# Building the convolution bands by columns, and reordering the loads and first factors of the head, in a fused convolution and FFN kernel

## The chip, the cores and the metric

The kernel runs on one core of one Trainium2 chip. The metric is device time in microseconds (us) of one execution; lower is better. PE is TensorE, DVE is VectorE, ACT is ScalarE, POOL is GpSimd and SP is SyncE; PE has its own row, PEld, for weight loads.

## The reference

`x` has shape (8, 3904, 192) and `weight` has shape (8 heads, 7 taps). Each head owns 24 of the 192 channels.

```python
w = softmax(weight, axis=-1)                      # per head, over the 7 taps
x_pad = 6 rows of zeros ahead of each of the 8 sequences
out[b, s, h, g] = sum_k w[h, k] * x_pad[b, s + k, h, g]
x = out.reshape(31232, 192)
h = ((x @ w1) * (x @ w2)) @ w3                    # w1, w2: 192 x 1024; w3: 1024 x 1024
return h @ w_out                                  # w_out: 1024 x 192; float32
```

## The kernel before

The 31232 tokens are handled as two streams of 15616 (`r` = 0, 1), 64 partitions each. A chunk `R` has `CH` = 512 tokens of each stream, so there are 31 chunks, the last one of 256; four chunks form a group and there are eight groups. The program is written in the order in which each engine executes it: there is no scheduler, and each engine's queue follows the order of the Python calls.

**Convolution.** A window is 64 input rows that give 58 outputs (`Q` = 64, `ST` = 58, `PAD` = 6). `conv` (L416) multiplies a window with a 64 x 64 band matrix per head, which holds the seven softmaxed taps on its diagonals; the bands lie in `Aband`. Windows come in blocks `b` of 6, 4, 8, 10, 8, 20, 20 and 14; `xb` holds a block's inputs, `convo` its outputs, and `xT` the transposed tokens that TensorE needs next. Blocks 0 to 4 are transposed on TensorE (`pe_transpose`, L470, and `joint_transposes`, L629), later ones go through `rows` in memory and are transposed by DMA. `EARLY` is 6 x 58 = 348, the tokens of block 0.

**FFN.** `wd[0]` and `wd[1]` hold w1 and w2 in bf16, twice, once for each stream's 64 partitions. For each of eight tiles `ft` of 128 columns, `first_factor` (L500) makes the factor a = x @ w1 (i = 0) and b = x @ w2 (i = 1) into a pair of PSUM banks. `first_cast` (L508, ACT) copies a to `asb`, `first_times` (L519, DVE) multiplies it with b into `abT`. w3 @ w_out is made once (`W_sb`, L590), and `second_product` (L551) multiplies `abT` with it. ACT copies the result to `osb` (L556), which a DMA stores (L566, L559).

**PSUM** is four pairs of banks in a list: `banks()` takes the first, `drained(p)` appends it again. A matmul into a pair waits for the copy that emptied it.

**The head**, up to about 40 us, in the order in which it is issued:

- SP loads the first quarter (256 columns) of both weights as float32 into `wfirst` (L176, two DMAs).
- POOL issues the input loads, which also convert to bf16: rows 1 to 5 of block 0 (L184), the first window's rows (L194, two DMAs of 58 rows), block 1 (L131, two), the second quarter of w1 and w2 (L181, two) and so on. Between these loads stand POOL's own operations: a select that makes `diag` (L188), a conversion of a part of `wfirst` (L198), and, as a DMA fills only partitions 0 to 63 of `wd`, copies of each quarter to partitions 64 to 127 (`copy_w`, L202).
- PE runs matmuls on zeros (`warm`, L218), six of 512 columns first.
- DVE and ACT make the softmax, PE spreads the taps over the partitions (L242, then L244 copies them).
- `band` (L259, L268) makes the bands in four steps of two heads: DVE writes a product of `diag` and the taps (128 x 448), 28 matmuls with `ident` add up its seven diagonals, and ACT or DVE copies the result to `Aband` (L602).
- ACT converts `wfirst` between these copies (L198, three times), POOL the fourth part.
- The convolution of block 0 follows (L416, L599), its transposes, the convolution of block 1, then `first_part(0, [0], 0, EARLY)`, the transposes of block 1, `first_part(0, [1], 0, EARLY)`, then tokens 348 to 511 of both tiles, and tiles 2 to 7 with the convolutions of blocks 2 to 4 between them.

**The tail**: in the last group `second_product` stores chunk 28 with one DMA per stream, chunk 29 with four, and the last chunk in parts.

Of the kernel before, what the change touches and what calls it, by code (L numbers as in the profile page):

```python
# [8 lines left out]
FP32 = mybir.dt.float32  # L9
BF16 = mybir.dt.bfloat16  # L10
AX = mybir.AxisListType
ALU = mybir.AluOpType
# [4 lines left out]
def kernel(  # L17
# [10 lines left out]
    nc = tc.nc  # L28
# [125 lines left out]
    wfirst = work.tile([Q, 2, NP, DFF // 4], FP32, tag="abT", bufs=GROUP, name="wfirst")  # L154
# [4 lines left out]
    half = const.tile([1, 3 * Q], BF16)  # L159
    ident = const.tile([128, 128], BF16)  # L160
    diag = const.tile([128, Q + PAD], BF16)
    nc.vector.memset(zeros, 0.0)
    nc.vector.memset(tiny, 0.0)
    nc.vector.memset(ones, 1.0)
    nc.vector.memset(xb0[:, 0, :], 0.0)
    nc.vector.memset(half, 0.0)
    nc.vector.memset(half[:, Q:2 * Q], 1.0)
    nc.vector.memset(ident, 0.0)
# [9 lines left out]
    def load_w(part):  # L178
        cs = slice(WC[part], WC[part + 1])
        for i in range(2):  # L180
            nc.gpsimd.dma_start(out=wd[i][0:Q, :, cs], in_=w_rows[i][:, :, cs])  # L181

    def load_x0(r):
        nc.gpsimd.dma_start(out=xb0[Q * r:Q * r + Q, 1:, :], in_=x_spans(r, 1, 2 * n0 - 1))  # L184

    load_x0(0)
    for p0 in (0, Q):
        nc.gpsimd.affine_select(  # L188
            out=diag[p0:p0 + Q], in_=ones[p0:p0 + Q].to_broadcast([Q, Q + PAD]),
            pattern=[[-1, Q + PAD]], compare_op=ALU.is_equal, fill=0.0, base=0,  # L190
            channel_multiplier=1)
    load_x0(1)
    for r in range(NS):
        nc.gpsimd.dma_start(out=xb0[Q * r + PAD:Q * r + Q, 0, :],  # L194
                            in_=x_rows[r * TS:r * TS + ST, :])
    load_x(1)
    def cast_w(i, r, f):
        f(out=wd[i][Q * r:Q * r + Q, :, 0:WC[1]], in_=wfirst[:, i])  # L198

    def copy_w(part, i, f):  # L200
        cs = slice(WC[part], WC[part + 1])
        f(out=wd[i][Q:128, :, cs], in_=wd[i][0:Q, :, cs])  # L202

    load_w(1)
    cast_w(1, 1, nc.gpsimd.tensor_copy)
    load_w(2)
    load_x(2)
    for i in range(2):
# [3 lines left out]
        copy_w(2, i, nc.gpsimd.tensor_copy)  # L212
    load_x(3)

    def warm(n):
        p, t = banks()
        for j in range(n):
            nc.tensor.matmul(t[:, j % 2, :], zeros, zeros[:, 0:1].to_broadcast([128, CH]),  # L218
                             start=True, stop=True)
        drained(p)  # L220

    warm(6)

    wmax = const.tile([1, H], FP32)
    wsum = const.tile([1, H], FP32)
    wrow = const.tile([1, H, K], BF16)
    wsb = const.tile([128, 2, 2, K], BF16)
# [3 lines left out]
    nc.scalar.activation(out=wall, in_=wall, func=ACT.Exp)  # L231
    nc.vector.tensor_copy(out=ident[0:Q, 0:Q], in_=diag[0:Q, 0:Q])
    nc.vector.reduce_sum(out=wsum, in_=wall, axis=AX.X)
    nc.vector.reciprocal(out=wsum, in_=wsum)
    nc.vector.tensor_tensor(
        out=wrow, in0=wall, in1=wsum.unsqueeze(2).to_broadcast([1, H, K]), op=ALU.mult)
    nc.vector.tensor_copy(out=ident[Q:128, Q:128], in_=diag[Q:128, 0:Q])
    pw, wbc = banks()
    wbc = wbc[:, 0, 0:H * K // 2].rearrange("p (g e k) -> p g e k", g=2, e=2)
    wrow = wrow.rearrange("p (g e a) k -> p g e a k", g=2, a=2)  # L240
    for a in range(2):
        nc.tensor.matmul(wbc, half[:, Q - Q * a:Q - Q * a + 128], wrow[:, :, :, a],  # L242
                         start=(a == 0), stop=(a == 1))
    nc.vector.tensor_copy(out=wsb, in_=wbc)  # L244
    drained(pw)
    warm(2)

    Aband = const.tile([128, 2, 2, 2, Q], BF16)

    def band_of(h, r):  # L250
        return Aband[Q * r:Q * r + Q, h // 4, (h % 4) // 2, int(h % 2 != r), :]

    d0 = diag[:, 0:1]
    taps = bass.AP(tensor=d0.tensor, offset=d0.offset,
                   ap=[list(d0.ap[0]), [1, K], [1, Q]])

    def band(g, e):
        c = slot([128, K, Q], BF16, "cprod")
        nc.vector.tensor_tensor(  # L259
            out=c, in0=taps, in1=wsb[:, g, e].unsqueeze(2).to_broadcast([128, K, Q]),  # L260
            op=ALU.mult)
        p, bps = banks()
        for k in range(K):
            for v in range(2):
                for r in range(2):
                    rs = slice(Q * r, Q * r + Q)
                    o = Q * (r ^ v)
                    nc.tensor.matmul(bps[o:o + Q, v, 0:Q], ident[rs, rs], c[rs, k, :],  # L268
                                     start=(k == 0), stop=(k == K - 1))
        return p, Aband[:, g, e], bps[:, :, 0:Q]  # L270


    shared, held, VHEADS = {}, [], (3, 4, 6, 7)

# [217 lines left out]
    def first_factor(R, i, fts, c0, c1):  # L492
        n, r0 = c1 - c0, (R * CH) % RING
        assert len(fts) * n <= CH
        q, p = banks()
        for e, ft in enumerate(fts):
            for k in range(NP):
                for r in range(NS):
                    rs = slice(Q * r, Q * r + Q)
                    nc.tensor.matmul(  # L500
                        p[:, r, e * n:e * n + n], wd[i][rs, k, ft * 128:(ft + 1) * 128],
                        xT[k][rs, r0 + c0:r0 + c1], start=(k == 0), stop=(k == NP - 1))
        return q, p[:, :, 0:len(fts) * n]
# [97 lines left out]
    def put(f, p, dst, src):  # L601
        f(out=dst, in_=src)  # L602
        drained(p)

    cast_w(0, 0, A)
    put(A, *band(0, 0))
    put(A, *band(0, 1))
    cast_w(0, 1, A)
    made = [band(1, 0), band(1, 1)]
    put(V, *made[0])  # L610
    put(V, *made[1])
    cast_w(1, 0, A)

    def move_all(p, moves, fs):
        for f, m in zip(fs, moves):
            move(f, m)
        drained(p)
# [38 lines left out]
    first_part(0, [0, 1], EARLY, CH)  # L656
    load_w3(0)
    for i in range(2):
# [87 lines left out]
    for p in SHARED:  # L746
# [76 lines left out]
```

## Time and profile before

| | |
|---|---|
| median of three runs | 514.25 us (513.17 to 515.23) |
| time of the profiled execution | 512.8 us |
| its span in the profile | 511.1 us |
| PE busy | 505.2 us (99%) |
| DVE, ACT, POOL busy | 421.5, 358.3, 340.1 us |
| the chain that ended last | PE 96%, DVE 2%, ACT 1% |

The page divides the span into engines and groups of instructions; a line's number, as in L500, is that of the kernel before. A row of the timeline has the start, the time that the merged instructions took, the engine, the line, what is written and read, how many there were, and in brackets how long the engine had been idle and what ended that. An engine's name with a q is its queue at an instruction that only issues.

### The profile page before, as it was taken

Reading aid. Unit: us, or ns where it says so; the run is one execution under the profiler, and the core shown is the slowest. Engines: PE = TensorE matmul, PEld = TensorE weight load, DVE = VectorE, ACT = ScalarE, POOL = GpSimd, SP = SyncE. Lnnn points to the kernel's source line nnn. Section 1 sums busy time; section 2 is a strip of 40 time slices with the busy share of each in tenths; the row PEclk is TensorE's granted clock in tenths of the full one; section 3 lists DMA queues with packets and bytes.
Section 4 is the critical chain, followed back from the end, with each engine's and each line's share of the span. In section 5 each row is a group of like instructions: output and inputs, shape, how many; then the busy total and the mean of one; then the engine's idle time right before and its main releaser. Section 6 shows DMA issues by size and latency. Waiting matters only on the chain.

```text
span 511.1 us, 13682 instructions
## 1 busy us (share of the span) xinstructions
PE 505.2 (99%) x5608; PEld 343.4 (67%) x5608; DVE 421.5 (82%) x482; ACT 358.3 (70%) x479; POOL 340.1 (67%) x437
## 2 busy tenths in 40 slices
PE   8999999999999999999999999999999999999997
PEld 4554798555985559855598555985559855597487
DVE  6889624999959999699998999989999899983970
ACT  6787645777857777477785777857778577765762
POOL 8601535449979999899985999969999594030000
PEclk9999999999999999999999999999999999999999
DMA  9999999995692989687926898467963683036104
GB/s 120 165 172 122 169 179 228 153 211 81 93 257 88 138 112 193 217 132 63 124 95 185 155 120 102 119 192 149 116 78 107 190 139 63 2 118 183 27 3 156
DMA packets 135188, 67.91 MB, mean 133 GB/s; under 512 B 99050, under 2 KB 133411, under 8 KB 135061
## 3 DMA queue, kind: packets, MB, share of 16 engines
q0 software_dynamic: 48720, 29.05, 40.1%
q1 hardware_dynamic: 86259, 37.89, 35.3%
q8 instruction: 44, 0.72, 0.6%
q14 instruction: 19, 0.16, 0.1%
q10 hardware_dynamic: 146, 0.10, 0.1%
HBM read 39.60 MB, written 36.56 MB: 149 GB/s over the span
## 4 chain that ended last, share of the span: by engine, by line
PE 96%; DVE 2%; ACT 1%; issue 0%; ACTq 0%; DVEq 0%
PE pairs L500 61%; PE pairs L551 32%; PE pairs L416 2%; PE pairs L590 1%; DVE abT L519 1%; ACT asb L508 1%; PE pairs L218 1%; DVE cprod L259 0%; PE pairs L629 0%; ACT convo L437 0%; PE pairs L470 0%; DVE xT L642 0%; DVE convo L599 0%; PE pairs L268 0%; ACT osb L556 0%
## 5 line engine op out<-in xcount | busy, mean ns | idle before, releaser
L519 DVE TENSOR_TENSOR abT<-asb,pairs 128x1024 bf16<-128x1024 bf16 (+1 forms) x245 | 298.0, 1217 | 31.3 <-ACT asb L508 14.1
L500 PE MATMUL pairs<-xT,wd 64*128 64x512 bf16 (+3 forms) x3000 | 319.4, 371 | 0.5 <-DVE xT L642 0.2
L508 ACT CAST asb<-pairs 128x1024 bf16<-128x1024 f32 (+1 forms) x245 | 247.3, 1009 | 66.7 <-PE pairs L500 66.6
L500 PEld LDWEIGHTS <-wd 64*128 64x128 bf16 x3000 | 164.9, 94 | 149.2 <-issue 1.4
L551 PE MATMUL pairs<-W_sb,abT 128*128 128x192 bf16 x1952 | 163.3, 246 | 0.0
L551 PEld LDWEIGHTS <-abT 128*128 128x128 bf16 x1952 | 160.4, 98 | 3.7 <-issue 3.7
L556 ACT COPY osb<-pairs 128x384 f32<-128x384 f32 x122 | 57.7, 476 | 73.1 <-PE pairs L551 72.1
L347 POOL TENSOR_TENSOR acc<-acc,term 128x480 f32<-128x480 f32 (+2 forms) x90 | 92.9, 1032 | 7.1
L344 POOL TENSOR_TENSOR term<-xv,wv 128x480 f32<-128x480 bf16 (+2 forms) x114 | 97.5, 856 | 0.0
L329 DVE SCALAR_TENSOR_TENSOR pairs<-xv,wv,pairs 128x480 f32<-128x480 bf16 (+2 forms) x120 | 76.6, 638 | 5.0 <-ACT pairs L327 1.6
L347 POOL TENSOR_TENSOR terms<-terms 128x480 f32<-128x480 f32 (+2 forms) x30 | 31.0, 1034 | 29.4 <-ACT terms L300 27.8
L437 DVE CAST convo<-pairs 128x672 bf16<-128x672 f32 (+9 forms) x29 | 20.4, 752 | 33.7 <-PE pairs L416 17.2
L338 POOL TENSOR_TENSOR acc<-xv,wv 128x480 f32<-128x480 bf16 (+2 forms) x18 | 15.7, 872 | 13.8 <-DMA xv<-in_x_dram 13.4
L350 POOL TENSOR_TENSOR y<-acc,term 128x240 bf16<-128x240 f32 (+7 forms) x48 | 22.8, 502 | 1.4
L300 ACT ACTIVATE terms<-xv,wv 128x480 f32<-128x480 bf16 (+2 forms) x36 | 20.6, 625 | 0.0
L332 DVE SCALAR_TENSOR_TENSOR y<-xv,wv,pairs 128x240 bf16<-128x240 bf16 (+2 forms) x48 | 18.1, 420 | 1.1
L384 POOL DMA_DIRECT2D rows<-y x10 | 5.7, 572 | 19.6 <-issue 17.5
L461 POOL DMA_DIRECT2D rows<-convo x10 | 6.0, 604 | 17.2 <-ACT convo L437 16.6
L131 POOL DMA_DIRECT2D xb<-in_x_dram x20 | 13.9, 721 | 3.4 <-PE pairs L590 2.7
L327 ACT ACTIVATE pairs<-xv,wv 128x480 f32<-128x480 bf16 (+2 forms) x24 | 14.0, 597 | 1.1 <-DVE y L332 1.1
L359 POOL DMA_DIRECT2D xb<-in_x_dram x20 | 14.7, 756 | 0.0
L279 POOL DMA_DIRECT2D xv<-in_x_dram x12 | 13.5, 1128 | 1.4 <-DMA rows<-convo 1.2
(70 smaller groups left out, 113.5 us busy)
## 6 DMA issues: line engine op xcount, KB each, us to landing
out_dram<-osb SPq DMA_DIRECT2D x50, 384.0 KB, 3.2
xv<-in_x_dram POOLq DMA_DIRECT2D x6, 768.0 KB, 9.6
out_dram<-osb POOLq DMA_DIRECT2D x8, 384.0 KB, 4.9
xv<-in_x_dram POOLq DMA_DIRECT2D x4, 672.0 KB, 13.7
xb<-in_x_dram POOLq DMA_DIRECT2D x16, 168.0 KB, 6.4
rows<-y POOLq DMA_DIRECT2D x3, 720.0 KB, 6.3
w3rows<-in_moe_w_dram POOLq DMA_DIRECT2D x2, 1024.0 KB, 12.1
xb<-in_x_dram POOLq DMA_DIRECT2D x8, 240.0 KB, 6.3
```

The lines of the kernel that those rows point to most:

```text
L300: nc.scalar.activation(out=term.rearrange("p (m g) -> p m g", g=G), in_=xv[:, k:k + W].rearrange("p s r c -> p (s r) c")[:, :, h * G:h * G ...
L329: f.scalar_tensor_tensor(out=flat, in0=xs(k), scalar=tap(k), in1=flat, op0=ALU.mult, op1=ALU.add)
L332: f.scalar_tensor_tensor(out=dst, in0=xv[:, 0:W, r, h * G + cs.start:h * G + cs.stop], scalar=tap(0), in1=by_row[:, :, r, cs], op0=ALU.mul ...
L344: f.tensor_tensor(out=term.rearrange("p (m g) -> p m g", g=G), in0=xs(k), in1=wide(k), op=ALU.mult)
L347: f.tensor_tensor(out=acc, in0=acc, in1=term, op=ALU.add)
L350: f.tensor_tensor(out=dst, in0=by_row[:, :, r, cs], in1=term[:, :, r, cs], op=ALU.add)
L437: f[e % len(f)](out=dst, in_=part)
L500: nc.tensor.matmul(p[:, r, e * n:e * n + n], wd[i][rs, k, ft * 128:(ft + 1) * 128], xT[k][rs, r0 + c0:r0 + c1], start=(k == 0), stop=(k == ...
L508: nc.scalar.copy(out=asb, in_=pa)
L519: nc.vector.tensor_tensor(out=dst, in0=asb, in1=pb, op=ALU.mult)
L551: nc.tensor.matmul(ops[:, (g - g0) * D:(g - g0) * D + D], ab[:, jt, r, g * 128:(g + 1) * 128], W_sb[:, jt, :], start=(jt == 0), stop=(jt = ...
L556: f(out=osb[:, g0:g0 + per, :].rearrange("p g d -> p (g d)"), in_=ops[:, 0:per * D])
```

## The change

**Bands by columns.** The eight heads' bands are made together. The taps, divided by their sum, are written twice into a row `wrow`; one matmul turns that row into a column on 128 partitions (two blocks of 64, each with 8 x 7 taps), and DVE multiplies it with a mask, `heads`, so that `tapcol` has in column h only the taps of head h. Columns 8 to 63 of `tapcol` are zeros. `shift` is a 64-row matrix whose columns, read from another start, move the taps down by one row. For each of the 58 output positions and both streams, one matmul of 64 columns gives that position's column of all eight bands: 29 x 2 x 2 = 116 matmuls. Then two copies, one of DVE (positions 0 to 28) and one of ACT (29 to 57), of 128 x 232 each, write `Aband`. `shift` and `heads` are made by two DVE reductions of `ident`, which POOL now makes directly with one select of 128 x 128. The product on DVE (L259, four of 128 x 448) is gone, and so are the four copies to `Aband`.

**Loads.** SP loads the first quarter of w1 alone, then the first window's rows of x as float32 into `xfirst` in four DMAs (48 and 10 rows for each stream); ACT converts them into `xb0`. The two DMAs of POOL for these rows are gone. The first quarter of w2 is loaded by POOL with conversion, behind block 1's x, and copied to partitions 64 to 127 by POOL behind the issue of the second quarter. `wfirst` of w1 is converted by ACT (stream 0) and by DVE (stream 1).

**Factors a first.** For tokens 0 to 347 the factors a of tiles 0 and 1 are both made before block 1's transposes; b of tile 0 and of tile 1 follow them.

**Warm-up.** Seven matmuls of 512 columns instead of six at the start, then one of 256 instead of two of 512, and two of 256 each after the bands and after block 0's convolution.

**Stores at the end.** Chunk 29 goes out in two DMAs per stream instead of four, and stream 1 of chunk 28 in two instead of one.

```diff
-    wfirst = work.tile([Q, 2, NP, DFF // 4], FP32, tag="abT", ...)
+    wfirst = work.tile([Q, NP, DFF // 4], FP32, tag="abT", ...)
+    xfirst = slot([128, D], FP32, "xfirst")
...
-    for i in range(2):
-        nc.sync.dma_start(out=wfirst[:, i], in_=w_rows[i][:, :, 0:WC[1]])
+    nc.sync.dma_start(out=wfirst, in_=w_rows[0][:, :, 0:WC[1]])
+    for r in range(NS):
+        for s0, s1 in ((0, 48), (48, ST)):
+            nc.sync.dma_start(out=xfirst[Q * r + PAD + s0:Q * r + PAD + s1],
+                              in_=x_rows[r * TS + s0:r * TS + s1, :])
...
     load_x0(0)
-    for p0 in (0, Q):
-        nc.gpsimd.affine_select(out=diag[p0:p0 + Q], ...)
+    nc.gpsimd.affine_select(out=ident, in_=ones.to_broadcast([128, 128]), ...)
     load_x0(1)
-    for r in range(NS):
-        nc.gpsimd.dma_start(out=xb0[Q * r + PAD:Q * r + Q, 0, :], ...)
     load_x(1)
+    load_w(0, (1,))
...
     load_w(1)
-    cast_w(1, 1, nc.gpsimd.tensor_copy)
+    copy_w(0, 1, nc.gpsimd.tensor_copy)
     load_w(2)
     load_x(2)
...
-    warm(6)
+    warm(7, CH)
...
+    nc.vector.reduce_max(out=shift[:, Q - 1:Q - 1 + K], in_=..., axis=AX.XY)
...
+    nc.vector.reduce_max(out=heads, in_=..., axis=AX.XY)
     pw, wbc = banks()
+    nc.tensor.matmul(wbc[:, 0, 0:H], wrow.rearrange("o a q -> o (a q)"), unit, ...)
+    nc.vector.tensor_tensor(out=tapcol[:, 0:H], in0=wbc[:, 0, 0:H], in1=heads, op=ALU.mult)
...
+    def make_bands(f0, f1):
+        p, bps = banks()
+        n = ST // 2
+        for s in range(n):
+            for i in range(2):
+                for r in range(NS):
+                    rs = slice(Q * i, Q * i + Q)
+                    t = i * n + s
+                    nc.tensor.matmul(
+                        bps[Q * r:Q * r + Q, i, s * H:s * H + Q],
+                        shift[rs, Q - 1 - t:2 * Q - 1 - t], tapcol[rs], ...)
+        for i, f in enumerate((f0, f1)):
+            f(out=Aband[:, :, i * n:i * n + n],
+              in_=bps[:, i, 0:n * H].rearrange("p (s h) -> p h s", h=H))
+        drained(p)
...
-    cast_w(0, 0, A)
-    put(A, *band(0, 0))
-    put(A, *band(0, 1))
-    cast_w(0, 1, A)
-    made = [band(1, 0), band(1, 1)]
-    put(V, *made[0])
-    put(V, *made[1])
-    cast_w(1, 0, A)
+    cast_w(0, A)
+    cast_w(1, V)
+    A(out=xb0[:, 0, :], in_=xfirst)
+    make_bands(V, A)
+    warm(2)
...
     move_all(*conv(0, 4, 4, ()), (A, A))
+    warm(2)
...
     first_tile(0)
-    first_part(0, [0], 0, EARLY)
+    a = [first_factor(0, 0, [ft], 0, EARLY) for ft in range(2)]
+    asb = first_cast(*a[0])
     joint_transposes(1)
-    first_part(0, [1], 0, EARLY)
+    for ft in range(2):
+        b = first_factor(0, 1, [ft], 0, EARLY)
+        first_times(0, [ft], 0, EARLY, asb, *b)
+        if ft == 0:
+            asb = first_cast(*a[1])
     first_part(0, [0, 1], EARLY, CH)
...
+    PIECES = {(NR - 2, r): 2 for r in range(NS)} | {(NR - 3, 1): 2}
...
-                           4 if R == NR - 2 else 1)
+                           PIECES.get((R, r), 1))
```

More of the change, by code (lines that the diff above doesn't have):

```diff
@@ L158 @@
     zeros = const.tile([128, 128], BF16)
-    half = const.tile([1, 3 * Q], BF16)
+    unit = const.tile([1, H], BF16)
     ident = const.tile([128, 128], BF16)
-    diag = const.tile([128, Q + PAD], BF16)
+    wrow = const.tile([1, 2, Q], BF16)
+    shift = const.tile([128, 2 * Q], BF16)
+    heads = const.tile([128, H], BF16)
+    tapcol = const.tile([128, Q], BF16)
+    Aband = const.tile([128, H, Q], BF16)
     nc.vector.memset(zeros, 0.0)
@@ L164 @@
     nc.vector.memset(ones, 1.0)
[L165 to L168, printed above, removed]
+    nc.vector.memset(xfirst, 0.0)
+    nc.vector.memset(unit, 1.0)
+    nc.vector.memset(wrow, 0.0)
+    nc.vector.memset(shift, 0.0)
+    nc.vector.memset(tapcol, 0.0)
+    nc.vector.memset(Aband[:, :, ST:Q], 0.0)
     nc.scalar.activation(out=tiny, in_=tiny, func=ACT.Exp)
@@ L213, with warm @@
     load_x(3)
-    def warm(n):
+    def warm(n, cols=CH // 2):
         p, t = banks()
         for j in range(n):
-            nc.tensor.matmul(t[:, j % 2, :], zeros, zeros[:, 0:1].to_broadcast([128, CH]),
-                             start=True, stop=True)
+            nc.tensor.matmul(t[:, j % 2, 0:cols], zeros,
+                             zeros[:, 0:1].to_broadcast([128, cols]), start=True, stop=True)
         drained(p)
-    warm(6)
+    warm(7, CH)
     wmax = const.tile([1, H], FP32)
     wsum = const.tile([1, H], FP32)
-    wrow = const.tile([1, H, K], BF16)
-    wsb = const.tile([128, 2, 2, K], BF16)
+    HK = H * K
+    blocks = ident[:, :].rearrange("p (a c) -> p a c", a=2)[:, :, 0:HK]
     nc.vector.reduce_max(out=wmax, in_=wall, axis=AX.X)
@@ L231 @@
     nc.scalar.activation(out=wall, in_=wall, func=ACT.Exp)
-    nc.vector.tensor_copy(out=ident[0:Q, 0:Q], in_=diag[0:Q, 0:Q])
+    nc.vector.reduce_max(out=shift[:, Q - 1:Q - 1 + K],
+                         in_=blocks.rearrange("p a (h k) -> p k a h", k=K), axis=AX.XY)
     nc.vector.reduce_sum(out=wsum, in_=wall, axis=AX.X)
@@ L235 @@
     nc.vector.tensor_tensor(
-        out=wrow, in0=wall, in1=wsum.unsqueeze(2).to_broadcast([1, H, K]), op=ALU.mult)
-    nc.vector.tensor_copy(out=ident[Q:128, Q:128], in_=diag[Q:128, 0:Q])
+        out=wrow[:, :, 0:HK].rearrange("o a (h k) -> o a h k", k=K),
+        in0=wall.unsqueeze(1).to_broadcast([1, 2, H, K]),
+        in1=wsum.unsqueeze(1).unsqueeze(3).to_broadcast([1, 2, H, K]), op=ALU.mult)
+    nc.vector.reduce_max(out=heads, in_=blocks.rearrange("p a (h k) -> p h a k", k=K), axis=AX.XY)
@@ L238 @@
     pw, wbc = banks()
[L239 to L244, printed above, removed]
+    nc.tensor.matmul(wbc[:, 0, 0:H], wrow.rearrange("o a q -> o (a q)"), unit,
+                     start=True, stop=True)
@@ L245 @@
+    nc.vector.tensor_tensor(out=tapcol[:, 0:H], in0=wbc[:, 0, 0:H], in1=heads, op=ALU.mult)
     drained(pw)
-    warm(2)
-    Aband = const.tile([128, 2, 2, 2, Q], BF16)
+    warm(1)
     def band_of(h, r):
[L251 to L261, printed above, removed]
-        p, bps = banks()
[L263 to L270, printed above, removed]
+        return Aband[Q * r:Q * r + Q, h, :]
```

20 lines of the change are left out of this document (9 added, 11 removed).

## The prediction

> **What bounds the kernel now.** I read the page's busy shares and chain first, then busy time by stretches, then the timeline of the first 20 us engine by engine, then DMA landings.
>
> ```profile
> PE 505.2 (99%) x5608; PEld 343.4 (67%) x5608; DVE 421.5 (82%) x482; ACT 358.3 (70%) x479; POOL 340.1 (67%) x437
> PE 96%; DVE 2%; ACT 1%; issue 0%; ACTq 0%; DVEq 0%
> ...
> 0.00:12.00 12.00, 10.17 (x225) 5.40 (x226) 8.15 (x29) 7.79 (x15) 10.67 (x21) 1.00 0.87 117
> 12.00:24.00 12.00, 11.75 (x178) 6.39 (x178) 10.31 (x13) 9.25 (x13) 8.83 (x14) 1.00 1.11 170
> 40.00:500.00 460.00, 460.00 (x4941) 315.91 (x4938) 389.05 (x427) 325.62 (x430) 318.64 (x400) 1.00 0.74 131
> 500.00:511.00 11.00, 7.52 (x92) 7.29 (x89) 0.36 (x1) 2.83 (x7) 0.00 (x0) 1.00 0.44 145
> ```
>
> In each stretch the columns are its length, then busy time of PE, PEld, DVE, ACT and POOL. From 40 to 500 us PE is never idle, and the change touches nothing there. PE idles 1.83 us in the first 12 us, 0.25 us in the next 12, and 3.48 us at the very end. So a gain must come out of the first 12 us or the tail. A loss can arise wherever the head makes PE wait anew: whatever delay stands at 40 us reaches the end whole, since nothing behind it has slack. POOL is busy for 10.67 of the first 12 us, which will matter.
>
> **The bands, step by step.**
>
> ```profile
> 1.07 1.46 PE L218 MATMUL pairs<-zeros 128*128 128x512 bf16 x3 [1.07 <-DVE ones L164]
> 1.07 2.74 PE L218 MATMUL pairs<-zeros 128*128 128x512 bf16 x6 [1.07 <-DVE ones L164]
> 3.02 0.20 DVE L233 TENSOR_REDUCE wsum<-wall 1x8 f32<-1x56 f32 x1 [0.25 <-ACT wall L231]
> 3.74 0.23 PE L242 MATMUL pairs<-wrow,half 1*128 1x28 bf16 x2
> 4.01 0.19 DVE L244 CAST wsb<-pairs 128x28 bf16<-128x28 f32 x1
> 4.23 2.23 DVE L259 TENSOR_TENSOR cprod<-diag,wsb 128x448 bf16<-128x448 bf16 x4
> 4.91 0.59 PE L268 MATMUL pairs<-cprod,ident 64*64 64x64 bf16 x28
> 6.51 0.41 PE pairs L268 x28
> 6.35 1.69 ACT L198 CAST wd<-wfirst 64x768 bf16<-64x768 f32 x2
> 6.98 0.29 DVE L602 CAST Aband<-pairs 128x128 bf16<-128x128 f32 x1 [0.24 <-PE pairs L268]
> 7.41 0.82 DVE L599 CAST convo<-pairs 128x384 bf16<-128x384 f32 x2
> 7.94 0.68 ACT L599 CAST convo<-pairs 128x192 bf16<-128x192 f32 x2
> 9.32 1.06 PE L500 MATMUL pairs<-xT,wd 64*128 64x348 bf16 x12
> ```
>
> The first three warm-up matmuls took 1.46 us and all six 2.74, so one more costs (2.74 - 1.46) / 3 = 0.43. The seventh starts at 1.07 + 6 x 0.43 = 3.65 and lets PE go at 4.08, where the tap matmul began at 3.74: 0.34 later. DVE's own way is longer too: the reductions for `shift` and `heads` and the doubled product add about three times 0.2 (L233's duration) to a path that ended at 3.7, but `heads` lies beside PE, so the taps are ready near 3.95 and the warm-up is what ends last. DVE read the taps 0.27 behind the matmul's start (3.74 to 4.01) and took 0.19; the new mask product does so from 4.35 to 4.54, and the first band matmul starts at about 4.6, against 4.91.
>
> The 2.23 us of L259, which sat on the path, go. There are 116 band matmuls of the size of L268's, instead of 112. Its first 28 took 0.59 and its last 28 took 0.41; take 0.2 off each for the last one's passage (two small ones of L242 took 0.23). That leaves 0.39 or 0.21 per 28, and 116 take 0.2 + 0.87 = 1.07 or 0.2 + 1.62 = 1.82. The rate changed between the two rows, so I take 1.5: the bands end at 6.1 (5.7 to 6.4). The copy of 128 columns took 0.29; for 232 it lies between that and 0.53, and the two L599 copies (576 columns in 0.82) put it near 0.4. `Aband` is whole at 6.5, where before its last part came at 6.98 + 0.29 = 7.27.
>
> Not all of this 0.77 is gained. Before, the first half of the convolution ran while the last bands were copied, so DVE could start on `convo` at 7.41, 0.14 behind the last band. Now it starts behind wait and 16 matmuls, about 0.5 later than `Aband`: 7.0. ACT gains more: it was held by L198 until 8.04 and now starts at 7.2 instead of 7.94. Transposes and `xT` copies keep their size, so the first L500 comes at about 8.85 instead of 9.32: **0.45 gained** (0.1 to 0.8).
>
> The first rows must be there by then. POOL's loads of rows 1 to 5 decide it as before:
>
> ```profile
> xb<-in_x_dram POOLq DMA_DIRECT2D x1, 120.0 KB, 3.8
> 2.83 0.73 POOL L184 DMA_DIRECT2D xb<-in_x_dram  x1
> 3.55 1.09 POOL L194 DMA_DIRECT2D xb<-in_x_dram  x2
> ```
>
> Stream 1's rows landed at 2.83 + 3.8 = 6.63, just where the new bands end, and half as much of `wfirst` goes ahead of them now, so they cost nothing. SP's four DMAs stand behind one `wfirst` DMA and have until then. ACT's conversion of 128 x 192 lies in its wait for the bands; the added warm-up pairs lie in waits of PE for copies.
>
> **Factors a first.** `wd[1]` is needed later, and DVE copies `xT` of block 1 before its first product.
>
> ```profile
> 10.75 0.88 DVE L519 TENSOR_TENSOR abT<-asb,pairs 128x696 bf16<-128x696 bf16 x1 [0.65 <-ACT asb L508]
> 12.05 4.91 PE L500 MATMUL pairs<-xT,wd 64*128 64x164 bf16 x60 [0.24 <-DVE xT L642]
> 13.82 1.01 ACT L508 CAST asb<-pairs 128x1024 bf16<-128x1024 f32 x1 [0.42 <-PE pairs L500]
> 16.35 1.01 ACT L508 CAST asb<-pairs 128x1024 bf16<-128x1024 f32 x1 [0.28 <-PE pairs L500]
> 17.68 2.76 PE L500 MATMUL pairs<-xT,wd 64*128 64x512 bf16 x24
> ```
>
> PE's 0.24 wait at 12.05 goes, but both products now end later on DVE (0.88 each), and b of tokens 348 to 511 needs the pair that the first empties. That gives back about 0.1: with the 0.45, tile 2 could start about 0.6 sooner. It started at about 12.9: ACT's cast at 13.82 came behind six matmuls (0.69 by the last row, 2.76 / 4) and 0.2 of passage. Tile 4, by its cast at 16.35, started at 15.45.
>
> **POOL's queue takes this back.** Tiles 2 and 3 need the second quarter on partitions 64 to 127, tiles 4 and 5 the third, tiles 6 and 7 the fourth.
>
> ```profile
> 2.29 0.60 POOL L188 TENSOR_SCALAR_AFFINE_SELECT diag<-ones 64x70 bf16<-64x70 bf16 x2
> 4.63 1.27 POOL L131 DMA_DIRECT2D xb<-in_x_dram  x2
> 5.88 1.27 POOL L181 DMA_DIRECT2D wd<-in_moe_w_dram  x2
> 7.20 0.82 POOL L198 CAST wd<-wfirst 64x768 bf16<-64x768 f32 x1
> 9.21 1.38 POOL L131 DMA_DIRECT2D xb<-in_x_dram  x2
> 12.11 1.23 POOL L181 DMA_DIRECT2D wd<-in_moe_w_dram  x2
> 13.34 1.60 POOL L202 COPY wd<-wd 64x768 bf16<-64x768 bf16 x2
> 14.88 1.44 POOL L131 DMA_DIRECT2D xb<-in_x_dram  x2
> DMA to landing us min/median/max: 3.1/4.1/4.6
> ```
>
> POOL never waited here. One select of 128 columns costs 0.30 to 0.55 against 0.60 for two of 70, so the issue of stream 1's rows still ends near 3.55, and block 1's x follows at 3.55 instead of 4.63: L194's 1.09 are gone. It ends at 4.82, the new load of w2's first quarter at 5.45, the second quarter's at 6.72. Then `copy_w(0, 1)` stands where L198 stood, and it **waits for a DMA that POOL issued only at 4.82**. The loads of `wd` took 3.1 to 4.6 to land, so it starts between 7.9 and 9.4. I take 8.6, under the median, as SP moves less ahead of it. Behind it are queued all later loads and copies. With 0.80 for a copy (1.60 / 2) it ends at 9.4, the third quarter's issue at 10.6 (1.23), block 2's x at 12.0 (1.38), the copies of the second quarter at 12.8 and 13.6, the fourth quarter's issue at 14.85, the copies of the third at 15.65 and 16.45.
>
> Set against PE: tile 2's a waits until about 12.85, as late as before, so **the 0.6 is gone**. Its b (12.9 + 0.69 = 13.6 before) gets its copy at 13.6. Tile 4's a (15.45) waits until 15.65 and its b (16.15) until 16.45: 0.3 late, and the fourth quarter's copies, behind another 1.44 of issue, come as late for tile 6. Products queued on DVE (busy 10.31 of these 12 us) may hide a part; I count it whole. **Head: 0.3 later** (0.6 sooner to 1.1 later, by the ends of the landing).
>
> **Tail.**
>
> ```profile
> 505.42 1.76 SPq L566 DMA_DIRECT2D out_dram<-osb  x3
> 507.33 0.35 SPq L559 DMA_DIRECT2D out_dram<-osb  x1
> 507.95 0.38 ACTq L559 DMA_DIRECT2D out_dram<-osb  x1
> ```
>
> SP was through with 505.42 + 1.76 = 507.18 when the last chunk's rows were ready, and the last store is ACT's. Fewer DMAs on SP shorten no wait that decides: 0 (0.2 sooner to 0.2 later).
>
> **Sum**: -0.6 + 0.6 + 0.3 + 0 = 0.3 us. The profiled execution, 512.8 us with 1.7 outside its span, would become 513.1. The median of three runs, 514.25, lies 1.45 higher; the same 0.3 on it gives **514.6 us**.
>
> **The rivals.**
>
> *POOL is in time.* If the quarter lands after 3.1, everything on POOL is 0.7 sooner: the second quarter's first copy ends at 12.1 and tile 2 starts at 12.3; the third's (14.95 and 15.75) hold tile 4 by 0.1 to 0.2. Net 0.4 to 0.6 sooner, 513.75 us. For it: less data ahead. Against it: the median is 4.1.
>
> *The landing is late*, slower than before clearly. At 4.6, `copy_w(0, 1)` starts at 9.4, all behind it shifts by 0.8 more, and b of tiles 4 and 6 is 1.1 late: 515.35 us. It decides from a start past 9.0. For it: block 1's x is now directly ahead of it.
>
> *DVE's cast holds POOL's issue.* The change puts a 64 x 768 float32 copy on DVE at about 4.55, when POOL issues block 1's x and w2. If POOL cannot issue meanwhile, its queue is later by up to that copy, 0.82 by POOL's own L198 row, unless the landing was bound by bandwidth anyway: 514.6 + 0.8 = 515.4 us at most. The trace of before speaks neither way: POOL's issues beside L259 (1.27 for two at 4.63) are as long as those later without it (1.23 at 12.11), but L259 is a product and no copy. The Trainium skill, "SBUF — State Buffer", section "SBUF: two separate sides", speaks for this rival: while a float32 copy within SBUF runs on VectorE in its two-port mode, GpSimd cannot write its DMA descriptors. By that rule the sum would be 1.1 instead of 0.3; no run here shows it yet.
>
> *PE stays at its slow rate longer.* Bands at 6.4, transposes and convolutions up to 0.5 longer; the 0.6 of cover that POOL's wait leaves takes this up, so 514.6 to 514.9 us. The rows show only that the rate rose between 4.91 and 6.51, and the granted clock is 1.00 throughout. The Trainium skill, "TensorE: Matmul & The Clock Gate", section "Part 1: The HAM clock gate", says that the rate doubles after about 3.4 us of activity by a window that runs freely, so the point may differ by run.
>
> **How the numbers follow.** Chances: the forecast 0.45, POOL in time 0.30, late landing 0.10, DVE's hold 0.08, slow PE or something unseen 0.07. The range goes from 513.65 (0.6 sooner) less 0.5 to 515.5 plus 0.5, since medians of runs that spread over 2 us carry about that: 513.1 to 516.0. A measurement of this kernel can tell about 0.5% from no change, 2.6 us; none of the cases reaches it, so within 0.5% gets 0.92. Faster gets 0.03; slower gets 0.05, for a wait that I don't see.
>
> **What would show it.** Right: L259 gone, bands done near 6.1, first L500 near 8.9, POOL idle ahead of the first `wd` copy (start 8.2 to 9.0), and PE waiting for POOL's copies at tiles 2, 4 or 6. PE's continuous stretch then ends as late as before. Wrong: POOL without a wait and tile 2 near 12.3 (a gain of half a microsecond), or any new idle time of PE behind 40 us.

## The result and the profile after

| | before | after |
|---|---|---|
| median of 22 runs each | 513.46 us (512.59 to 515.56) | 514.96 us (513.53 to 517.01) |
| time of the profiled execution | 512.8 us | 514.4 us |
| its span | 511.1 us | 512.7 us |

The ratio after to before is 1.0026 (95% interval 1.0014 to 1.0038), about 1.3 us slower. That is within half a per cent, and the median is 0.4 us above the 514.6 forecast. Chance helped: the forecast stood on a median of three runs, 514.25, which is 0.8 above that of 22. As a difference, 0.3 us was forecast and 1.3 came. Line numbers of the changed kernel are a few higher: the seven warm-up matmuls are L225, the bands L266 and L270, the first factors L501, POOL's copies L209.

From the page of the profile after, the busy line and the chain that ended last:

```profile
PE 506.1 (99%) x5615; PEld 344.8 (67%) x5615; DVE 420.2 (82%) x480; ACT 356.9 (70%) x477; POOL 338.8 (66%) x435
PE 94%; DMA 3%; POOL 1%; ACT 1%; DVE 1%; issue 0%; POOLq 0%; ACTq 0%
```

DMA and POOL, which had no share of the chain before, now have 3% and 1%. The same stretches of the kernel after, columns as before:

```profile
0.00:12.00 12.00, 10.48 (x244) 6.16 (x245) 6.84 (x27) 6.50 (x13) 7.80 (x16) 1.00 0.71 91
12.00:24.00 12.00, 11.22 (x162) 5.20 (x159) 9.43 (x12) 8.14 (x10) 10.97 (x17) 1.00 1.10 148
40.00:500.00 460.00, 459.35 (x4931) 316.23 (x4929) 390.07 (x428) 325.44 (x429) 318.46 (x401) 1.00 0.75 131
500.00:512.70 12.70, 9.36 (x114) 9.13 (x111) 0.36 (x1) 3.67 (x8) 0.00 (x0) 0.96 0.48 157
```

DVE has 1.31 us less to do in the first 12 us and POOL is busy for 7.80 instead of 10.67: it waits. PE loses 0.53 in the second stretch, where tile 2 starts, and 0.65 behind 40 us, where it had not been idle at all. The tail's idle time is as before (12.70 - 9.36 = 3.34, before 3.48).

The timeline of PE of the kernel after:

```profile
4.61 1.77 PE L266 MATMUL pairs<-tapcol,shift 64*64 64x64 bf16 x116
9.15 1.06 PE L501 MATMUL pairs<-xT,wd 64*128 64x348 bf16 x12
13.64 4.34 PE L501 MATMUL pairs<-xT,wd 64*128 64x512 bf16 x35 [0.60 <-POOL wd L209]
40.47 3.84 PE L501 MATMUL pairs<-xT,wd 64*128 64x512 bf16 x34
```

The bands start at 4.61, as forecast, and the product L259 is gone. The first factors start at 9.15 (before 9.32). But tile 2 starts at 13.64, where the forecast's working had 12.9 for before, and PE waited for a copy of POOL to start it. The last row is the first factors behind the transposes of block 4; from there PE is busy almost without a break. I call its start **the start of the long stretch**. The next row is the same place in the kernel before, from its timeline of PE:

```profile
39.47 6.87 PE L500 MATMUL pairs<-xT,wd 64*128 64x512 bf16 x62
```

So the head is 1.0 us longer (40.47 against 39.47). The time is about 1.3 us longer, by the ratio's interval 0.7 to 2.0, so the head can account for it. POOL's timeline of the kernel after shows where that is from:

```profile
3.32 1.25 POOL L131 DMA_DIRECT2D xb<-in_x_dram  x2
4.53 1.89 POOL L191 DMA_DIRECT2D wd<-in_moe_w_dram  x3
9.38 0.82 POOL L209 COPY wd<-wd 64x768 bf16<-64x768 bf16 x1 [2.97 <-DMA wd<-in_moe_w_dram]
10.15 1.23 POOL L191 DMA_DIRECT2D wd<-in_moe_w_dram  x2
11.37 1.38 POOL L131 DMA_DIRECT2D xb<-in_x_dram  x2
12.75 1.60 POOL L209 COPY wd<-wd 64x768 bf16<-64x768 bf16 x2
15.51 1.60 POOL L209 COPY wd<-wd 64x768 bf16<-64x768 bf16 x2
```

POOL issues block 1's x, then w2's first quarter at 4.53, then the second quarter, and stands still for 2.97 us until the first one has landed. The loads of the third quarter and of block 2's x come only behind that copy, and the second quarter's copies behind these, at 12.75. The chain that ended last, in order of time, runs through this wait, and through a second one:

```profile
4.53 4.71 DMA wd<-in_moe_w_dram
...
90.94 9.12 DMA xT<-rows
100.11 30.82 PE pairs L501 x284
```

The second is PE's wait of 0.65 us near 100 us for tokens that come transposed by DMA. It is absent from the first profile of before.

### The profile page after: what moved, and what is told of

Same layout as the page of the kernel before. It is cut to its first block, busy times and chain, and to the rows that moved or that the text cites. A ratio compares the mean times of both kernels' runs of the same rounds, so it can differ in the third digit from the quotient of the medians.

```text
span 512.7 us, 13693 instructions
## 1 busy us (share of the span) xinstructions
PE 506.1 (99%) x5615; PEld 344.8 (67%) x5615; DVE 420.2 (82%) x480; ACT 356.9 (70%) x477; POOL 338.8 (66%) x435
## 4 chain that ended last, share of the span: by engine, by line
PE 94%; DMA 3%; POOL 1%; ACT 1%; DVE 1%; issue 0%; POOLq 0%; ACTq 0%
PE pairs L501 59%; PE pairs L552 32%; DMA xT<-rows 2%; PE pairs L417 1%; PE pairs L591 1%; DMA wd<-in_moe_w_dram 1%; POOL xb L131 1%; DVE abT L520 0%; ACT asb L509 0%; POOL wd L209 0%; PE pairs L627 0%; POOL xb L194 0%; POOL wd L191 0%; ACT convo L438 0%; POOL ident L197 0%
## 5 line engine op out<-in xcount | busy, mean ns | idle before, releaser
L501 PE MATMUL pairs<-xT,wd 64*128 64x512 bf16 (+3 forms) x3000 | 320.4, 371 | 1.7 <-DMA xT<-rows 0.7
L501 PEld LDWEIGHTS <-wd 64*128 64x128 bf16 x3000 | 166.0, 94 | 150.3 <-issue 2.4
```

The lines of the kernel that those rows point to most:

```text
L501: nc.tensor.matmul(p[:, r, e * n:e * n + n], wd[i][rs, k, ft * 128:(ft + 1) * 128], xT[k][rs, r0 + c0:r0 + c1], start=(k == 0), stop=(k == ...
```

## The experiments

The theory: PE's head is longer because POOL waits for w2's first quarter with the other copies and loads behind it. Rivals: the bands run at the slow rate and cost the time; the wait near 100 us is the cost; or the factors' new order is. The experiments take the parts one by one.

**Move only the copy** (from after). The copy stands behind the next loads, so that they do not wait with it:

```diff
     load_w(1)
-    copy_w(0, 1, nc.gpsimd.tensor_copy)
     load_w(2)
     load_x(2)
+    copy_w(0, 1, nc.gpsimd.tensor_copy)
```

> The changed kernel with one line moved: POOL's copy of w2's first quarter stands behind the issue of the third quarter and of block 2's x, instead of ahead of them. Theory (POOL's wait of 2.97 us for that quarter's landing holds every later load and copy): the landing stays at about 9.2, POOL works through and waits under 0.5 us, the second quarter's copies end near 10.9 and 11.7 instead of 13.6 and 14.3, tile 2 starts near 12.3 instead of 13.6, PE's continuous stretch starts at 39.0 (40.5 in the changed kernel, 39.5 before), and the wait for transposed tokens near 100 us goes: 1.5 to 2.1 us less than the changed kernel, 0.1 to 0.7 us less than before. Rival (the time is lost in the bands or the warm-up, and POOL's wait is covered): as the changed kernel, 1.3 us over before.

Measured: 0.9986 (0.9969 to 1.0004), median 513.24 beside 514.06 of before. The timeline of this kernel, POOL and PE:

```profile
4.52 3.09 POOL L191 DMA_DIRECT2D wd<-in_moe_w_dram  x5
...
9.27 0.82 POOL L209 COPY wd<-wd 64x768 bf16<-64x768 bf16 x1 [0.28 <-DMA wd<-in_moe_w_dram]
10.61 1.59 POOL L209 COPY wd<-wd 64x768 bf16<-64x768 bf16 x2 [0.53 <-DMA wd<-in_moe_w_dram]
39.32 6.87 PE L501 MATMUL pairs<-xT,wd 64*128 64x512 bf16 x62
```

The load lands at about the same time, but POOL's wait is 0.81 instead of 2.97, the copies of the second quarter start 2.1 us sooner, and the long stretch starts at 39.32 instead of 40.47. The whole loss of the head goes with the order of one copy. Not all of the theory came: the stretch does not start at 39.0, and the wait near 100 us has not gone (0.45).

**Only that load, in the kernel before.** w2's first quarter comes by POOL, behind block 1's x, and is copied by POOL; all else is the kernel before:

```diff
-    for i in range(2):
-        nc.sync.dma_start(out=wfirst[:, i], in_=w_rows[i][:, :, 0:WC[1]])
+    nc.sync.dma_start(out=wfirst[:, 0], in_=w_rows[0][:, :, 0:WC[1]])
...
     load_x(1)
+    load_w(0, (1,))
...
-    cast_w(1, 1, nc.gpsimd.tensor_copy)
+    copy_w(0, 1, nc.gpsimd.tensor_copy)
...
-    cast_w(1, 0, A)
```

> The kernel before with only this part of the change: w2's first quarter is loaded by POOL behind block 1's x and copied by POOL where its conversion of that quarter stood. Theory (POOL's wait): the load is issued near 5.9, lands near 10.6, POOL waits 3 us or more there, b of tile 0 starts at 11.5 instead of 9.8 and tile 2 near 14.9 instead of 12.9; 1.5 to 2.8 us over before, with a wait for transposed tokens near 100 us. Rival (the load costs nothing by itself): within 0.3 us of before.

Measured: 1.0038 (1.0019 to 1.0058). Its timeline:

```profile
10.46 0.82 POOL L202 COPY wd<-wd 64x768 bf16<-64x768 bf16 x1 [2.69 <-DMA wd<-in_moe_w_dram]
11.33 1.04 PE L500 MATMUL pairs<-xT,wd 64*128 64x348 bf16 x5 [0.56 <-POOL wd L202]
42.19 4.06 PE L500 MATMUL pairs<-xT,wd 64*128 64x512 bf16 x36
```

With this part alone the head is 2.7 us longer: the load is issued 1.4 us later than in after, and even b of tile 0 waits for the copy. But the waits are not all of the 2.7. Behind them PE's granted clock stood at 0.50 from 11.37 to 14.78 us, with PE busy throughout (last section), and half of these 3.41 us, 1.7, can be the clock. So the run shows that this load alone brings POOL's wait and a longer head, and not what the rest of the change buys back. The wait expected near 100 us did not come.

**Only the factors' order, in the kernel before.**

```diff
-    first_part(0, [0], 0, EARLY)
+    a = [first_factor(0, 0, [ft], 0, EARLY) for ft in range(2)]
+    asb = first_cast(*a[0])
     joint_transposes(1)
-    first_part(0, [1], 0, EARLY)
+    for ft in range(2):
+        b = first_factor(0, 1, [ft], 0, EARLY)
+        first_times(0, [ft], 0, EARLY, asb, *b)
+        if ft == 0:
+            asb = first_cast(*a[1])
```

> The kernel before with only the factors a of tiles 0 and 1 made first. Theory: PE's wait of 0.24 us at 12.05 goes and the second pair's emptying gives back 0.1; tile 2 starts 0.1 to 0.2 us sooner than 12.9 at most, and the time is 0 to 0.2 us under before, which the interval will not separate from none. Rival (the new order makes DVE's products of tiles 0 and 1 end later and so holds PE): tile 2 later than 12.9 and the time 0.2 to 0.6 us over before.

Measured: 0.9986 (0.9965 to 1.0007). The long stretch starts at 39.47, where it was. PE's 0.24 us wait at 12.05 has become one of 0.18 at 12.49, with the first factors at 9.40 instead of 9.32:

```profile
12.49 2.76 PE L500 MATMUL pairs<-xT,wd 64*128 64x164 bf16 x32 [0.18 <-DVE abT L519]
```

**w2's first quarter by SP again** (from after), behind the first rows. POOL's copy becomes a cast, and ACT has one more, behind the bands:

```diff
+    nc.sync.dma_start(out=wfirst[:, 1], in_=w_rows[1][:, :, 0:WC[1]])   # behind xfirst
...
-    load_w(0, (1,))
...
-    copy_w(0, 1, nc.gpsimd.tensor_copy)
+    cast_w(1, nc.gpsimd.tensor_copy, 1)
...
     make_bands(V, A)
+    cast_w(0, A, 1)
```

> The changed kernel with w2's first quarter loaded by SP again, behind the first rows of x, and converted by ACT (behind the bands) and POOL. Theory (POOL's wait): that wait goes or falls under 1 us, the second quarter's copies end near 11 and 12, tile 2 starts near 12.4, 1.2 to 2.0 us less than the changed kernel, so within 0.5 us of before or less. ACT's added conversion, 0.83, costs up to 0.3 at block 0's convolution. Rival (bands and warm-up): as the changed kernel, 1.3 us over before.

Measured: 1.003 (1.0012 to 1.0048), long stretch from 41.61. The gain that the theory expected did not come, but this does not test the change without POOL's wait. POOL still waited 2.24 us for this quarter, until 8.05. ACT's added cast waited for it too, until 7.94, and delayed block 0's copies behind it. Then the clock fell. PE's timeline of this kernel:

```profile
9.04 0.71 PE L471 MATMUL pairs<-ident,convo 128*128 128x128 bf16 x6 [0.75 <-ACT convo L600]
10.25 1.92 PE L501 MATMUL pairs<-xT,wd 64*128 64x348 bf16 x12
```

The twelve matmuls that make a of tiles 0 and 1 took 1.92 instead of 1.06, at a granted clock of 0.50 (last section).

**The same, with both quarters ahead of the first rows on SP.**

```diff
     nc.sync.dma_start(out=wfirst[:, 0], in_=w_rows[0][:, :, 0:WC[1]])
+    nc.sync.dma_start(out=wfirst[:, 1], in_=w_rows[1][:, :, 0:WC[1]])
     # xfirst, four DMAs, follows
```

> The changed kernel with w2's first quarter loaded by SP ahead of the first rows of x, as in the kernel before, and converted by ACT (behind the bands) and POOL. Theory (POOL's wait for w2's first quarter is what the change lost in the head): POOL's wait at that place falls from 2.97 us to under 0.5, the second quarter's copies end near 11 and 12, block 0's convolution starts at 6.9 to 7.2, tile 2 starts at 12.3 to 12.7, PE's continuous stretch at 39.0 to 39.5, 0.8 to 1.5 us less than the changed kernel. Rival (PE's granted clock falls whenever ACT's conversion holds the copies of block 0's convolution): the clock of the first 12 us under 1.00 again, tile 2 at 13.5 or later, and the time at that of the changed kernel or over it.

Measured: 1.0056 (1.0036 to 1.0076), long stretch from 43.18. Its timelines of ACT and PE:

```profile
8.08 0.35 ACT L608 CAST xb<-xfirst 128x192 bf16<-128x192 f32 x1 [2.81 <-DMA xfirst<-in_x_dram]
8.74 0.70 PE L417 MATMUL pairs<-xb,Aband 64*64 64x72 bf16 x32 [2.57 <-ACT Aband L270]
11.50 1.92 PE L501 MATMUL pairs<-xT,wd 64*128 64x348 bf16 x12
```

PE's wait is named for ACT's `Aband` copy, but that copy stood in ACT's queue behind the conversion of the first rows, which waited 2.81 us for their DMA, until 8.08. So with two `wfirst` DMAs ahead of them the rows came too late. POOL itself waited 0.73 us here and its copies of the second quarter were done by 11.5, and no gain shows: the convolution started 1.8 us later than in after (8.74 against 6.96), and PE then ran at half its clock until 15.1. The theory's gain failed and the rival's lower clock came, though it was the rows' load that held PE first.

**One warm-up matmul less** (the kernel with the copy moved, `warm(7, CH)` to `warm(6, CH)`).

> The changed kernel with POOL's copy moved as in the first experiment, and with six matmuls of 512 columns at the start instead of seven. Theory (the seventh lies on the path of the taps): the tap matmul starts at 3.8 instead of 4.17, the first band matmul at 4.3 instead of 4.61, the bands end 0.3 sooner at the same rate of 13.3 ns for each, tile 2 at 12.1 to 12.3 and PE's continuous stretch at 39.0 to 39.3; the time differs from the first experiment's by 0.4 us at most. Rival (the seventh keeps PE busy enough to reach its fast rate in time): the granted clock falls below 1.00 in the first 24 us and tile 2 comes later than 12.4.

Measured: 1.0039 (1.0017 to 1.0061). The bands started at 4.25 and the first factors at 8.81, but in the profiled run w2's first quarter landed at 11.0, where the kernel with seven had it at 9.1, with the issue at the same 4.5 in both. PE's timeline:

```profile
11.05 0.32 PE L501 MATMUL pairs<-xT,wd 64*128 64x348 bf16 x1 [0.74 <-DMA wd<-in_moe_w_dram]
12.02 1.48 PE L501 MATMUL pairs<-xT,wd 64*128 64x348 bf16 x23 [0.65 <-POOL wd L209]
```

Over twelve runs this kernel is slower than the kernel before, by 0.2 to 0.6%, and the one profile does not tell why: its granted clock stayed at 1.00, against the rival, and the landing was late. It shows that b of tile 0 is the next to wait when the load is late. Whether the seventh matmul has to do with the landing stays open.

**Both kernels once more, one profile each.**

> The kernel before once more, for a second profile. Theory (the wait for chunk 5's transposed tokens near 98 us, 0.65 us in the changed kernel's profile, 0.45 and 0.33 in those of the first and fourth experiment, depends on when the transposes happen to land and not on this change): a wait between 0 and 0.5 us there. Rival (the change brought it): none, as in the first profile. The head as before: continuous stretch at 39.5.

> The changed kernel once more, for a second profile. Theory: POOL waits 2.5 to 3.2 us for w2's first quarter, the second quarter's copies end at 13.3 to 13.8 and 14.1 to 14.6, PE's continuous stretch starts at 40.2 to 40.6, and a wait of 0 to 0.8 us for transposed tokens near 99 us. Rival (the first profile was a chance): POOL's wait under 2 us and the stretch at 39.5.

Measured: 514.03 us for before and 514.06 us for after, both with a span of 512.3. PE's waits between 85 and 130 us, first before, then after, and PE's timeline, first before, then after:

```profile
PE pairs L500 <- DMA xT<-rows: 1.1, 1, 1.1
```
```profile
PE pairs L501 <- DMA xT<-rows: 0.5, 1, 0.5
```
```profile
9.18 1.06 PE L500 MATMUL pairs<-xT,wd 64*128 64x348 bf16 x12
39.34 6.87 PE L500 MATMUL pairs<-xT,wd 64*128 64x512 bf16 x62
```
```profile
8.86 1.06 PE L501 MATMUL pairs<-xT,wd 64*128 64x348 bf16 x12
13.47 0.82 PE L501 MATMUL pairs<-xT,wd 64*128 64x512 bf16 x6 [0.72 <-POOL wd L209]
40.33 6.00 PE L501 MATMUL pairs<-xT,wd 64*128 64x512 bf16 x54
```

The wait for transposed tokens is in the kernel before too, and longer, so the change did not bring it. In this profile of after the bands ran faster, the first factors started at the forecast 8.86, 0.3 sooner than in the first profile, and tile 2 still waited for POOL until 13.47. The long stretch starts at 40.33 against 39.34 in the second profile of before: 1.0 again.

**w2's first quarter ahead of block 1's x** (from after, the copy in its place).

```diff
-    load_x(1)
     load_w(0, (1,))
+    load_x(1)
```

> The changed kernel with one order undone: POOL issues the load of w2's first quarter ahead of block 1's x, not behind it. The copy that waits for it stays where the change has it. Theory (POOL's wait for this load decides the head): the load is issued 1.2 us sooner, near 3.3; the loads of POOL's queue landed one behind the other in the profiles so far (6.9, 7.4, 7.9 and then 9.1 for this one), so it lands near 8.1, POOL waits 1.6 us instead of 3.0, the second quarter's copies end at 12.3 and 13.1 instead of 13.6 and 14.35, tile 2 starts near 12.5, and PE's continuous stretch starts at 39.4 to 39.7 instead of 40.4. Against that stands block 1's x: if landings go by the order in the queue it lands near 9.1 and holds the convolution of block 1, which started at 8.72, by 0.4; if each load has its own 4.0 to 4.5 us it lands at 8.6 and holds nothing. Ratio to the kernel before 0.998 to 1.001. Rival (where the load stands does not matter, as its landing is bound by all that is moved before it): POOL waits as long as before, ratio 1.0026 again.

Measured: 0.9991 (0.9965 to 1.0017), long stretch from 39.34. POOL:

```profile
3.32 0.65 POOL L191 DMA_DIRECT2D wd<-in_moe_w_dram  x1
7.50 0.82 POOL L209 COPY wd<-wd 64x768 bf16<-64x768 bf16 x1 [1.06 <-DMA wd<-in_moe_w_dram]
```

A load issued 1.2 us sooner lets POOL go 1.9 us sooner, and the head is as short as before's. Its profiled run has a span of 512.5 all the same, as PE waited 1.5 us for transposed tokens, most of it near 184 us. The rival, that the load's place does not matter, falls.

**Both orders moved**, the load ahead of block 1's x and the copy behind the next loads; run twice.

> The kernel in which POOL's copy of w2's first quarter stands behind the loads of the fourth quarter and of block 2, and in addition the load of that quarter ahead of block 1's x. Theory (once the copy stands later POOL's wait is under 1 us, so the load's place has nothing left to give): tile 2 near 12.9 and the continuous stretch at 39.3 to 39.7, as with the copy alone moved; block 1's x later by one load can only hold its convolution. Ratio 0.998 to 1.001. Rival (the rest of POOL's wait, 0.8 us, still costs time): the stretch starts at 38.7 to 39.0 and the ratio is 0.997 or less.

> The kernel with both orders moved (copy later, load of w2's first quarter ahead of block 1's x) once more, as its ratio to the kernel before was 0.9978 with an interval up to 1.0004. Theory (it differs from the kernel before only by a head that is 0.1 to 0.4 us shorter, and by how long PE then waits near 98 us for transposed tokens, 0 to 1.1 us in all profiles so far): 0.997 to 1.000. Rival (nothing of it reaches the end): 0.9995 to 1.002. PE's continuous stretch from 39.2 in both.

Measured: 0.9978 (0.9951 to 1.0004) and 0.998 (0.9955 to 1.0004). The long stretch starts at 39.19 and 39.53. The first lies between the theory's range (from 39.3) and the rival's (up to 39.0), and the second is no sooner than before's (39.47 and 39.34). So the two profiles show no head that would carry what the ratio leans by, if that is real. Block 1's x is now what is late; PE in the first run:

```profile
8.76 0.43 PE L417 MATMUL pairs<-xb,Aband 64*64 64x48 bf16 x31 [0.20 <-DMA xb<-in_x_dram]
```

In the second run the same row starts at 9.10 and waited 0.36.

**The copy alone moved, once more.**

> The kernel with POOL's copy moved later once more, for its distance to the kernel before, which was 0.9986 with an interval that held 1. Theory (the wait of POOL was all that the change cost, and its bands gain nothing that reaches the end): 0.998 to 1.0005, the stretch of PE at 39.3. Rival (without the wait the change gains its 0.4 us of bands): 0.997 to 0.9992.

Measured: 1.0001 (0.9977 to 1.0026). In its profile the bands were quick:

```profile
4.61 1.14 PE L266 MATMUL pairs<-tapcol,shift 64*64 64x64 bf16 x116
8.77 1.06 PE L501 MATMUL pairs<-xT,wd 64*128 64x348 bf16 x12
39.01 5.35 PE L501 MATMUL pairs<-xT,wd 64*128 64x512 bf16 x48
```

Here the bands' gain reaches the long stretch: 0.3 to 0.5 sooner than in the two profiles of before, with a span of 510.3, the shortest of all. The median shows none of it; over 12 runs the times went from 511.97 to 516.74. Both versions lean to the kernel before's time or a little under it, and none is shown to beat it.

**All profiles together.** The column of the wait is what PE's busy time lacks between 40 and 500 us, nearly all of it for transposed tokens. The last column is the span less the two columns ahead of it.

| kernel | long stretch from | wait | span | rest |
|---|---|---|---|---|
| before | 39.47 | 0 | 511.1 | 471.6 |
| before, again | 39.34 | 1.07 | 512.3 | 471.9 |
| after | 40.47 | 0.65 | 512.7 | 471.6 |
| after, again | 40.33 | 0.53 | 512.3 | 471.4 |
| copy later | 39.32 | 0.54 | 511.5 | 471.6 |
| copy later, again | 39.01 | 0 | 510.3 | 471.3 |
| load ahead of x | 39.34 | 1.50 | 512.5 | 471.7 |
| both orders | 39.19 | 0.27 | 510.9 | 471.4 |
| both orders, again | 39.53 | 0.05 | 511.1 | 471.5 |
| factors' order alone | 39.47 | 0.32 | 511.4 | 471.6 |
| w2 by POOL alone | 42.19 | 0 | 514.0 | 471.8 |
| w2 by SP | 41.61 | 0.88 | 514.3 | 471.8 |
| w2 by SP, first | 43.18 | 0 | 515.0 | 471.8 |
| six warm-up matmuls | 40.65 | 0.47 | 512.7 | 471.6 |

Two numbers account for every span within 0.6 us: when the head ends, and how long PE waits for transposed tokens. This wait stands near 100 us in most profiles that have it, and near 184 us in three: 1.35 us with the load ahead of x, 0.88 with w2 by SP, 0.27 with both orders. What sets it was not tried; it goes from 0 to 1.07 with one and the same kernel.

## Why the prediction was right, and where it was not

**The mechanism was right: POOL's queue takes the gain back.** The copy that waits for its own load, with all later loads and copies queued behind it, is the cost. The longer head goes when the copy is moved, and it goes when the load is issued sooner. POOL's wait comes when that load alone is put into the kernel before.

**Its size was not.** The step is "I take 8.6, under the median, as SP moves less ahead of it". The load was issued at 4.53, 0.3 sooner than worked out, but took 4.71 us instead of 3.8, and the copy started at 9.38. That is the case which the prediction called late landing, from a start past 9.0, with a chance of 0.10. It gave 1.1 us over before, and 1.0 came in the head (0.3 was forecast for the likeliest case). The place was another, too: PE waited for POOL at tile 2 (0.60 us, in the second profile 0.72), and not at tiles 4 and 6, where the forecast had its 0.3. The nearest row was the longest landing, 4.6, and not the median. In the kernel before, it belongs to the first `wd` load that POOL issued directly behind block 1's x, at 5.88; the two issued at 7.97 and 8.6 landed in 3.1 to 3.2. The changed kernel has its load in that place. The DMA issues of the kernel after, in its first 20 us (KB each, median us to landing):

```profile
xb<-in_x_dram POOLq DMA_DIRECT2D x2, 120.0 KB, 3.9
xb<-in_x_dram POOLq DMA_DIRECT2D x2, 96.0 KB, 4.3
```

Those are blocks 0 and 1, 432 KB, all ahead of the load. With the load ahead of block 1's two it landed in 4.0 us, and POOL's wait fell from 2.97 to 1.06.

**The bands.** The start at 4.6 was right, and so was the bound on 116 matmuls, 1.07 to 1.82: the rows show 1.14 to 1.77 in the same place of different runs. I took 1.5. The first factors came at 9.15 or 8.86 instead of 8.85, so the gain of 0.45 was 0.17 or, against the second profile of before (9.18), 0.32. It mattered in neither, as POOL's wait stands behind it. A term that the prediction put at nothing held part of the gain, ACT's conversion of the first rows. In the second profile the bands ended 0.6 us sooner than in the first, but the convolution started only 0.25 sooner (6.71 against 6.96):

```profile
6.06 0.35 ACT L608 CAST xb<-xfirst 128x192 bf16<-128x192 f32 x1 [0.68 <-DMA xfirst<-in_x_dram]
6.71 0.45 PE L417 MATMUL pairs<-xb,Aband 64*64 64x72 bf16 x32 [0.60 <-ACT Aband L270]
```

ACT waited for the rows' load until 6.06, and its copy of `Aband`, for which PE waited, stood behind the conversion.

**Factors a first** was given some 0.15 of the 0.6 by which tile 2 could start sooner. Alone it moved the long stretch by nothing.

**Two rivals.** PE at its slow rate was there in the first profile of after (1.77), and cost little under POOL's cover, as the prediction had it: the long stretch starts 0.14 later than in the second profile, where the bands took 1.18. DVE's cast holding POOL's issues did not show. DVE's timeline of the kernel after:

```profile
4.59 0.95 DVE L205 CAST wd<-wfirst 64x768 bf16<-64x768 f32 x1
```

The cast ran from 4.59 to 5.54, and POOL's three issues from 4.53, shown above, took 1.89, 0.63 each, as much as the 1.27 for two in before. The Trainium skill, "SBUF — State Buffer", section "SBUF: two separate sides", makes that hold a matter of VectorE's two-port mode; at 0.95 us, no shorter than POOL's own 0.82 for the same shape, nothing speaks for this cast having run in it, though no run shows its mode.

**The tail** shows no change, as forecast: PE's idle time there is 3.34 us against 3.48. **"PE is never idle from 40 to 500 us"** was one profile's luck: the second profile of before lacks 1.07 us there. With it falls the step "whatever delay stands at 40 us reaches the end whole": 1.0 us of a longer head gave equal spans in the second pair of profiles, as the other wait was shorter by half of it and the rest lay in the remainder.

## What to carry to other kernels

On an engine that issues loads in order, a copy that waits for a load takes every later load with it; put the loads first and the copy where its data are sure to be there. When a wait is costed by the landing of a load, take the row of a load that stands behind as much data in the same queue, not the median of all. One profile that shows no wait is not proof that there is none: profile the unchanged kernel twice before building on "never idle".

## What the hardware showed that was not expected

A short idle time of PE can halve its clock for longer than it lasted. The traces keep records of the clock that was granted to PE. With both quarters on SP it was 1.00 from 4.87 us and 0.50 from 8.28 to 15.11. With one quarter behind the rows it was 1.00 from 6.32 and 0.50 from 9.73 to 13.14. With only w2's first quarter moved to POOL it was 1.00 from 4.54 and 0.50 from 11.37 to 14.78. Each of these spans is 3.41 us long or twice that. So I cut the time of each profile into stretches of 3.41 us from its first record. These are the three stretches ahead of a fall, in the same order, and one of the kernel with six warm-up matmuls (length, PE's busy time and matmuls, granted clock; the last two columns are the DMA's):

```profile
4.87:8.28 3.41, 1.30 (x117) 1.00 1.42 178
```
```profile
6.32:9.73 3.41, 2.16 (x54) 1.00 0.87 138
```
```profile
7.95:11.37 3.42, 2.11 (x50) 1.00 0.61 68
```
```profile
4.72:8.13 3.41, 2.40 (x141) 1.00 1.20 126
```

PE was idle for 2.11, 1.25 and 1.31 us in the three, and for 1.01 in the last, behind which the clock stayed at 1.00. In all 14 profiles no stretch up to about 495 us with 1.07 us or less of idle time was followed by a fall. The Trainium skill, "TensorE: Matmul & The Clock Gate", section "Part 1: The HAM clock gate", has the half clock after an idle window of about 3.4 us; the idle times here were shorter, so the measurement decides.

The 116 band matmuls began at 4.61 in every profile with seven warm-up matmuls, and their time goes with where the first record of full clock begins: 1.77 us where that is at 6.40 (after), 1.35 at 5.19 (both orders), 1.18 at 4.73 (after, again) and 1.14 at 4.64 (copy later, again). The 1.00 that the views print for the time ahead of the first record is no reading of the clock. In the kernel before the first record begins at 5.86, between the rows of 4.91 and 6.51 from which the prediction read that the rate rose.

And w2's first quarter, in the same place of POOL's queue, took 4.5 to 4.8 us to land in the four profiles with seven warm-up matmuls and 6.5 in the one with six.
